# Attention beside two feed-forward layers: block differences and output sums issued at other points, loads moved, and the softmax of the later heads done by ScalarE per head

## The chip, the core and the metric

One NeuronCore of a Trainium2 chip runs one program. The metric is the device time of one execution in microseconds (us). Engines are named as the profile names them: PE (TensorE matmuls), PEld (its weight loads), DVE (VectorE), ACT (ScalarE), POOL (GpSimd), and SP, whose queue issues the DMAs of this kernel in program order.

## The reference

Chunked attention with 4 batches, 8 heads, 768 positions, head size 64. Each chunk of 32 queries sees 8 memory slots, 16 positions to the left, its own 32 and 8 to the right: 64 slots. Then two feed-forward layers over 3072 tokens with 512 features and 2048 hidden values.

```python
scores = scale * np.matmul(q_c, k_full.transpose(0, 1, 3, 2))
scores = scores - np.max(scores, axis=-1, keepdims=True)
a = np.exp(scores)
a = a / (np.sum(a, axis=-1, keepdims=True) + 1e-09)
out[:, :, c_start:c_end] = np.matmul(a, v_full)
...
h = x @ w_in;  r = np.maximum(h, 0.0);  x = (r * r) @ w_out        # first layer
...
h = x @ w_in;  g = h * np.tanh(softplus(h));  y = g @ w_out        # second layer
```

## The kernel before

**Blocks and steps.** The tokens are cut into three blocks of 1024 (`NSB`), and each layer's 2048 hidden values into eight slices (`NQ`). A step is one block times one slice, so there are 48 of them: steps 0 to 23 are the first layer, 24 to 47 the second, eight to a block. All large matrix products use a seven-product scheme (Strassen-Winograd) over 2x2 blocks: instead of eight block products there are seven, and the blocks are first combined by sums and differences (`B11`, `B21`, `B12`, `B22` give `T1` to `T4`). Every operand is split into a rounded high part and a low part, so a block product is six matmuls of 128x512.

**What a step issues.** `step(s)` writes seven products of `x` with the first weight matrix (P1, P6, P5, P2, P7, P4, P3, six matmuls each, `product`, L474) and, between them, the products of the step before with the second weight matrix: eight `unit` groups of six matmuls (L525) in the first layer, seven `product2` groups of six (L560) in the second. After each group `rest()` (L677) issues what is planned for that point. A step of the first layer has 15 such points, numbered here (step, point); point 0 follows P1, 1 P6, 2 P5, 3 and 4 units 0 and 1, 5 P2, 6 P7, 7 to 9 units 2 to 4, 10 P4, 11 P3, 12 to 14 units 5 to 7.

**PSUM and who reads it.** P1 and P2 share a bank, P6, P7 and P4 a second, P5 and P3 a third. ACT copies the result of P1 (`u1`, L735), DVE adds it to that of P6 (`u2`, L744) before P7 may add to the bank, and to that of P7 (`u3`, L763) before P4; L765, L771 and L776 make three results for the activations. P2 may start when `u1` has been copied. ACT does the activation and the rounding (L493 to L503), POOL the low part (L494). `unit` results are added to `y_t` by DVE (L549; by ACT at the first slice of a block, L547), and those of `product2` to `m_t` (L558, L581).

**Attention beside the steps.** Four pairs of 128 queries belong to each block. Pairs 0 to 3 run before step 0 (`early(p)`), pairs 4 to 7 beside steps 0 to 7, pairs 8 to 11 beside steps 8 to 15, by `plan_attention` (L638): scores at point 0 of the pair, softmax at 1 and 2, exponentials at 3, `normalize` at 5, transposes at 12, copies of them by ACT at 13, values at 16, `sums_x` (POOL) at 18 and `store_x` at 22. A pair starts 25 points after the one before it in steps 0 to 7 and 19 after it in steps 9 to 15 (L882). Softmax is a maximum and a subtraction on DVE (L369, L370), one exponential of 128x512 on ACT for each half (L376), and sums on DVE (L380). `p`'s buffer is `xt0`, `k`'s `at0`, that of `v` and `stage` is `at1`.

**Between the layers.** When the last slice of a block of the first layer is done, `sums_y` (L615) stores `B11`, `B21`, `B22` and makes `T1` to `T4` by four DVE subtractions of 128x1024 in a row (L628), which are stored too. It stands behind steps 8, 16 and 24. At step 7, 15 and 23 `load_x` reads the next block's operands and `split_x` splits them (L275, L277). In the second layer seven block sums of 128x1024 on DVE (`combine`, L586, by the list `SUMS`) make the outputs of a block: two in its last step and five in the first step of the next, at the points where `done` (L717) names them. The seven blocks of `m_t` live in `y0`, `y1` and three other buffers; each block of tokens takes new ones.

**Queues.** DMAs are issued by SP, and `later(...)` keeps a store until the next `flush()`. An instruction that waits holds up all that stands behind it on its engine, SP included.

## Time and profile before

| | |
|---|---|
| time, median of 3 runs (lowest to highest) | 1129.05 us (1128.75 to 1133.09) |
| the profiled execution, its own time | 1126.08 us |
| span of its trace, first to last instruction | 1124.2 us |
| PE busy, share of the span | 1061.5 us, 94% |
| DVE / ACT / POOL busy | 898.6 / 561.6 / 430.5 us |
| granted TensorE clock, mean | 0.987 |
| chain that ended last: PE, DVE, DMA, ACT | 65%, 14%, 6%, 3% |
| DMA | 324.94 MB, mean 289 GB/s |

PE's busy time counts matmuls that overlap, and a matmul that waits in a filled pipeline still counts, so the stretches in which PE stood idle, and what ended them, tell more than the share. A granted clock of 1.00 is 2.4 GHz.

### The profile page before, as it was taken

Reading aid. Unit: us, or ns where it says so; the run is one execution under the profiler, and the core shown is the slowest. Engines: PE = TensorE matmul, PEld = TensorE weight load, DVE = VectorE, ACT = ScalarE, POOL = GpSimd, SP = SyncE. Lnnn points to the kernel's source line nnn. Section 1 sums busy time; section 2 is a strip of 40 time slices with the busy share of each in tenths; the row PEclk is TensorE's granted clock in tenths of the full one; section 3 lists DMA queues with packets and bytes.
Section 4 is the critical chain, followed back from the end, with each engine's and each line's share of the span. In section 5 each row is a group of like instructions: output and inputs, shape, how many; then the busy total and the mean of one; then the engine's idle time right before and its main releaser. Section 6 shows DMA issues by size and latency. Waiting matters only on the chain.

```text
span 1124.2 us, 19766 instructions
## 1 busy us (share of the span) xinstructions
PE 1061.5 (94%) x7478; PEld 872.3 (78%) x7478; DVE 898.6 (80%) x1170; ACT 561.6 (50%) x879; POOL 430.5 (38%) x327
## 2 busy tenths in 40 slices
PE   5779999897799999999999999999999999999997
PEld 5758787785677887888888878888878888778885
DVE  5686889969756766578999767988888888978888
ACT  2458555546544554647656555443354444444331
POOL 1215233232223333223322244546454554545552
PEclk9998999999989999999999999999999999999999
DMA  9556867777989898969999968989979889797441
GB/s 354 216 186 269 308 228 275 259 265 268 369 316 319 306 333 298 336 237 381 374 345 328 361 225 292 316 312 324 401 247 319 308 307 371 272 315 227 158 155 75
DMA packets 192125, 324.94 MB, mean 289 GB/s; under 512 B 13344, under 2 KB 151072, under 8 KB 188192
## 3 DMA queue, kind: packets, MB, share of 16 engines
q1 hardware_dynamic: 192032, 323.69, 80.9%
q8 instruction: 60, 0.98, 0.3%
q14 instruction: 33, 0.27, 0.1%
HBM read 231.62 MB, written 92.01 MB: 288 GB/s over the span
## 4 chain that ended last, share of the span: by engine, by line
PE 65%; DVE 14%; DMA 6%; issue 4%; ACT 3%; POOL 1%; SPq 0%; DVEq 0%; ACTq 0%; POOLq 0%
PE banks L480 29%; PE banks L535 16%; PE banks L570 15%; DVE m L558 3%; PE banks L416 1%; PE banks L346 1%; DVE r L521 1%; DMA w_d<-hi 1%; DMA w2s<-w_d 1%; DVE y L549 1%; DMA w1s<-w_d 1%; DVE ty L628 1%; DVE val L157 1%; DVE val L158 1%; DVE val L154 1%
## 5 line engine op out<-in xcount | busy, mean ns | idle before, releaser
L480 PE MATMUL banks<-x,w1s 128*128 128x512 f32 x2016 | 502.2, 396 | 19.1 <-DVE u L763 7.3
L494 POOL TENSOR_TENSOR g<-r,g 128x512 fp32r<-128x512 f32 x206 | 289.6, 1412 | 523.1 <-ACT g L493 434.6
L480 PEld LDWEIGHTS banks<-x,w1s 128*128 128x128 f32 x2016 | 382.3, 191 | 104.4 <-DVE u L763 9.0
L535 PE MATMUL banks<-g,w2s 128*128 128x512 f32 x1152 | 279.7, 394 | 6.9 <-DVE y L549 6.7
L535 PEld LDWEIGHTS banks<-g,w2s 128*128 128x128 f32 x1152 | 216.7, 190 | 55.7 <-DVE y L549 8.4
L570 PE MATMUL banks<-g,w2s 128*128 128x512 f32 x966 | 239.0, 390 | 1.2 <-DVE m L558 0.6
L570 PEld LDWEIGHTS banks<-g,w2s 128*128 128x128 f32 x966 | 180.6, 188 | 41.9 <-DVE m L558 2.3
L558 DVE TENSOR_TENSOR m<-banks,m 128x1024 f32<-128x1024 f32 x144 | 173.3, 1218 | 30.5 <-PE banks L570 27.5
L493 ACT CAST g<-r 128x512 fp32r<-128x512 f32 x206 | 127.0, 621 | 31.0 <-DVE r L521 23.7
L549 DVE TENSOR_TENSOR y<-banks,y 128x512 f32<-128x512 f32 x168 | 111.4, 682 | 25.7 <-PE banks L535 25.4
L494 POOL TENSOR_TENSOR g<-more,g 128x512 fp32r<-128x512 f32 x55 | 81.8, 1492 | 77.8 <-ACT g L493 63.2
L499 ACT ACTIVATE r<-r 128x512 f32<-128x512 f32 x72 | 45.4, 631 | 69.5 <-DVE r L771 46.1
L503 ACT ACTIVATE r<-r 128x512 f32<-128x512 f32 x48 | 30.3, 632 | 75.8 <-DVE r L765 38.4
L213 ACT CAST hi<-val 128x1024 fp32r<-128x1024 f32 (+1 forms) x32 | 30.4, 951 | 71.4 <-DVE val L158 42.3
L500 ACT ACTIVATE r<-r 128x512 f32<-128x512 f32 x96 | 60.7, 633 | 3.1
L154 DVE TENSOR_SCALAR val<-val 128x512 f32<-128x512 f32 x64 | 36.7, 573 | 24.4 <-ACT val L147 24.4
L346 PE MATMUL banks<-k,q 64*32 64x64 f32 x1536 | 39.4, 255 | 16.8 <-DMA k<-k_dram 10.1
L346 PEld LDWEIGHTS banks<-k,q 64*32 64x32 f32 x1536 | 33.4, 125 | 21.5 <-issue 18.2
L158 DVE SCALAR_TENSOR_TENSOR val<-raw,val 128x512 uint32<-128x512 uint32 x64 | 47.3, 738 | 2.2
L735 ACT COPY u<-banks 128x512 f32<-128x512 f32 x48 | 27.9, 581 | 41.1 <-PE banks L480 41.0
L386 POOL TENSOR_TENSOR p<-p,sum 128x512 f32<-128x512 f32 x22 | 25.6, 1186 | 57.8 <-DVE sum L383 23.3
L416 PE MATMUL banks<-pt,v 64*64 64x32 f32 x1536 | 35.1, 249 | 11.3 <-ACT pt L404 9.8
(72 smaller groups left out, 991.4 us busy)
## 6 DMA issues: line engine op xcount, KB each, us to landing
w1s<-w_d SPq DMA_DIRECT2D x280, 256.0 KB, 5.5
w2s<-w_d SPq DMA_DIRECT2D x229, 256.0 KB, 5.4
raw<-w_dram SPq DMA_DIRECT2D x64, 512.0 KB, 5.1
w_d<-w1s SPq DMA_DIRECT2D x8, 1792.0 KB, 7.1
x<-xs_d SPq DMA_DIRECT2D x14, 1024.0 KB, 10.7
k<-k_dram SPq DMA_DIRECT2D x24, 512.0 KB, 7.3
v<-v_dram SPq DMA_DIRECT2D x24, 512.0 KB, 8.7
xt<-xt_d SPq DMA_DIRECT2D x21, 512.0 KB, 7.3
```

The costliest lines, as they stand in the source:

```text
L154: nc.vector.tensor_scalar(out=val, in0=val, scalar1=LIMIT, scalar2=-LIMIT * NEGATIVE, op0=ALU.min, op1=ALU.max)
L158: nc.vector.scalar_tensor_tensor(out=vb, in0=low, scalar=29, in1=vb, op0=ALU.logical_shift_right, op1=ALU.bitwise_or)
L346: nc.tensor.matmul(out=s4[32 * c:32 * c + 32, j, hp, :], lhsT=q_t[p][r0:r0 + 64, j, hp, 32 * c:32 * c + 32], rhs=k_t[p][r0:r0 + 64, j, hp, ...
L416: nc.tensor.matmul(out=x_ps[par][64 * h2:64 * h2 + 64, o:o + 32], lhsT=v_t[p][j][r0:r0 + 64, h2, a, c, :], rhs=pt_t[p][r0:r0 + 64, h2, j, ...
L480: nc.tensor.matmul(out=ps, lhsT=w[:, a, f:f + 128], rhs=x[:, xi, c, kk, :], start=start and i == 0, stop=stop and i == len(order) - 1, ski ...
L493: nc.scalar.copy(out=g[:, 0], in_=r)
L494: nc.gpsimd.tensor_tensor(out=g[:, 1], in0=r, in1=g[:, 0].bitcast(FP32), op=ALU.subtract)
L500: nc.scalar.activation(out=r, in_=r, func=ACTF.Square)
L535: nc.tensor.matmul(out=ps, lhsT=w[:, a, blk(f), d % 2 * 128:d % 2 * 128 + 128], rhs=g_t[s, (f, t)][:, c, :], start=i == 0, stop=i == len(o ...
L549: nc.vector.tensor_tensor(out=y, in0=ps, in1=y, op=ALU.add)
L558: engine.tensor_tensor(out=to, in0=in0, in1=in1, op=ALU.add)
L570: nc.tensor.matmul(out=bank(first + d), lhsT=w[:, a, 128 * d:128 * d + 128], rhs=g[:, c, :], start=i == 0, stop=i == 2)
```

## The change

- **Softmax of pairs 4 to 11.** DVE still takes the maximum, then makes a small tile of -scale x maximum (128x8). The subtraction, the single exponential per half and the DVE sums go; ACT does eight exponentials of 128x64 per half, straight from PSUM, with the maximum as bias and the sum as a second result. Pairs 0 to 3 keep the old form.
- **Its points.** The second half's exponentials move to point 4, `normalize` to 6, the load of `v` to 8. The pairs start 24 points apart in steps 0 to 6, and 20 apart from point (8, 10) on; their loads of `q` and `k` stand at (8, 0) and (8, 1) instead of (9, 1).
- **Between the layers.** `sums_y` is replaced by `plan_sums`: stores of `B11` and `B21` at points 5 and 9 of the block's last step, `T1` at 13, `T2`, `T4` and `T3` at points 0, 1 and 3 of the next step. `T4` and `T3` are made in place in `y`; `T1` and `T2` go to `at1`, and `at0` is no longer used. The blocks of the first layer share one pair of `y` buffers.
- **Second layer.** The block sums 5 and 6 stand one and two products later in a block's first step. In the last step sum 6 goes to POOL behind product `T3`, sum 1 moves ahead to product `T2`, and the others stand two each behind `T2`, `T1` and `T4`. The blocks `T3`, `T2`, `T1`, `T4` of `m_t` keep their buffers from block to block.
- **Weights.** The second half's rounding and its split (`r`, `l`) of the second layer's weights stand one point later in steps 8 to 14.

```diff
     def softmax(p, h2):
...
+        nc.vector.tensor_reduce(out=mx, in_=s8, axis=AX.X, op=ALU.max)
+        if early(p):
+            nc.vector.tensor_tensor(
+                out=p_t[p][:, h2], in0=s8, in1=mx.unsqueeze(2).to_broadcast([128, 8, SLOTS]), op=ALU.subtract
+            )
+        else:
+            m_neg[p, h2] = sp.tile([128, 8], FP32, tag="mneg", name="mneg")
+            nc.vector.tensor_scalar(out=m_neg[p, h2], in0=mx, scalar1=-scale, scalar2=None, op0=ALU.mult)
...
     def exps(p, h2):
...
+        m = m_neg.pop((p, h2))
+        for i in range(8):
+            nc.scalar.activation(
+                out=pr[:, i], in_=s8[:, i], func=ACTF.Exp, scale=scale, bias=m[:, i:i + 1],
+                accum_out=r_t[p][:, h2, i:i + 1],
+            )
...
-            y_t[sb, t] = pool.tile([128, KD, NB], FP32, tag=f"y{t}", name="y")
+            y_t[sb, t] = y_t[sb - 1, t] if sb else pool.tile([128, KD, NB], FP32, tag=f"y{t}", name="y")
...
-            3: lambda: (exps(p, 0), exps(p, 1), load_k(p + 1) if (p + 1) % PSB else None),
-            5: lambda: (normalize(p), load_v(p) if p > PSB else None),
+            3: lambda: (exps(p, 0), load_k(p + 1) if (p + 1) % PSB else None),
+            4: lambda: exps(p, 1),
+            6: lambda: normalize(p),
+            8: lambda: load_v(p) if p > PSB else None,
...
+        s = (sb + 1) * NQ
+        at(s, 5, lambda: later(d[:, B11], blocks()[0]))
+        at(s, 9, lambda: later(d[:, B21], blocks()[1]))
+        at(s, 13, first)
+        at(s + 1, 0, second)
+        at(s + 1, 1, fourth)
+        at(s + 1, 3, third)
...
-                for n in {T2: (0,), T1: (1, 2, 3), T4: (4, 6, 5)}.get(blk, ()):
-                    combine(sb, *SUMS[n])
+                for n in {T3: (6,), T2: (0, 1), T1: (2, 3), T4: (4, 5)}.get(blk, ()):
+                    combine(sb, *SUMS[n], engine=nc.gpsimd if n == 6 else nc.vector)
...
-                for n in {B11: (3,), B22: (4,), B21: (5,), T3: (6,)}.get(blk, ()):
+                for n in {B11: (3,), B22: (4,), T3: (5,), T1: (6,)}.get(blk, ()):
...
-                plan_w(NQ + n, 0, e, "Aa|D|d|RS|s|L||||r|l", lambda e, i: round_w2(e, i, "xt2"), split_w2, "val")
+                plan_w(NQ + n, 0, e, "Aa|D|d|RS|s|L|||||r|l", lambda e, i: round_w2(e, i, "xt2"), split_w2, "val")
...
-            start, first, period = ((0, 4, 25), (NQ + 1, 8, 19))[sb]
+            start, first, period = ((0, 4, 24), (NQ, 10, 20))[sb]
```

The first place is ACT in step 0, where pair 4's exponentials stand between the activation behind P7 and the rounding of the second weights. Lines are those of each kernel: L376 before is L389 now, L499 is L516. Before:

```order
L499 ACTIVATE r<-r 128x512
L500 ACTIVATE r<-r 128x512
L493 CAST g<-r 128x512
L376 ACTIVATE p<-p 128x512 x2
L195 CAST w2s<-val 128x1024
L499 ACTIVATE r<-r 128x512
```

Now:

```order
L516 ACTIVATE r<-r 128x512
L517 ACTIVATE r<-r 128x512
L510 CAST g<-r 128x512
L389 ACTIVATE p,sum<-banks,mneg 128x64 x16
L195 CAST w2s<-val 128x1024
L516 ACTIVATE r<-r 128x512
```

Sixteen short instructions stand where two were, ahead of the same rounding and activation.

The second place is DVE over the end of step 8 and the start of step 9: the subtractions (L628, now L673), the weight decoding (L154 to L158) and `u2` (L744, now L791). Before:

```order
L628 TENSOR_TENSOR ty<-y 128x1024
L628 TENSOR_TENSOR ty<-y,ty 128x1024
L628 TENSOR_TENSOR ty<-y 128x1024
L628 TENSOR_TENSOR ty<-y,ty 128x1024
L154 TENSOR_SCALAR val<-val 128x512
L157 TENSOR_SCALAR val<-val 128x512
L158 SCALAR_TENSOR_TENSOR val<-raw,val 128x512
L744 TENSOR_TENSOR u_3107<-banks,u_3093 128x512
```

Now (L566 is the addition to `y`, L399 and L400 are pair 8's `normalize`, which waits for ACT's sums):

```order
L673 TENSOR_TENSOR ty<-y 128x1024
L566 TENSOR_TENSOR y<-banks,y 128x512 x2
L673 TENSOR_TENSOR ty<-y,ty 128x1024
L154 TENSOR_SCALAR val<-val 128x512
L157 TENSOR_SCALAR val<-val 128x512
L158 SCALAR_TENSOR_TENSOR val<-raw,val 128x512
L399 TENSOR_SCALAR sum<-sum 128x16
L400 RECIPROCAL sum<-sum 128x16
L673 TENSOR_TENSOR y<-y,ty 128x1024
L791 TENSOR_TENSOR u_3264<-banks,u_3243 128x512
```

One of the four subtractions moved into step 8, two stay ahead of `u2`, the fourth stands behind it, and the two operations of `normalize` came in ahead of `u2`.

The third place is DVE in steps 33 and 41: the block sums (L558 `m<-m`, now L575) around `u3` (L763, now L810). Before:

```order
L558 TENSOR_TENSOR m<-m 128x1024 x3
L763 TENSOR_TENSOR u_7923<-banks,u_7838 128x512
L765 TENSOR_TENSOR more<-banks,u_7923 128x512
L558 TENSOR_TENSOR m<-m 128x1024
```

Now:

```order
L575 TENSOR_TENSOR m<-m 128x1024 x2
L810 TENSOR_TENSOR u_8024<-banks,u_7941 128x512
L812 TENSOR_TENSOR more<-banks,u_8024 128x512
L575 TENSOR_TENSOR m<-m 128x1024
```

Two sums instead of three stand ahead of `u3`.

## Rows read from the trace of the kernel before

**Rows 1.** Stretches: start:end us, length, busy us by engine, clock, DMA share, GB/s.

```profile
535.40:555.80 20.40, 20.40 (x92) 16.90 (x91) 19.07 (x32) 14.42 (x23) 7.70 (x6) 1.00 1.02 376
61.40:264.90 203.50, 187.93 (x1761) 152.23 (x1762) 169.11 (x265) 118.48 (x187) 66.70 (x54) 0.97 0.72 261
264.90:473.30 208.40, 194.59 (x1825) 159.13 (x1824) 143.21 (x226) 108.65 (x173) 64.80 (x56) 0.97 0.89 313
288.80:324.80 36.00, 28.06 (x235) 22.41 (x234) 23.43 (x34) 17.74 (x30) 6.79 (x5) 0.86 1.02 379
637.40:1086.70 449.30, 442.54 (x1940) 362.80 (x1939) 378.68 (x381) 201.99 (x315) 229.51 (x159) 1.00 0.83 291
1086.70:1124.20 37.50, 30.06 (x133) 24.58 (x131) 31.23 (x29) 7.77 (x13) 12.07 (x8) 0.96 0.15 56
```

**Rows 2.** PE in order of time, steps 0 to 8: start, us, matmuls [idle before <-ended by].

```profile
84.37 2.93 PE L480 MATMUL banks<-x,w1s 128*128 128x512 f32 x6 [4.09 <-DVE r L771]
...
137.28 0.30 PE L416 MATMUL banks<-pt,v 64*64 64x32 f32 x2 [1.89 <-ACT pt L404]
...
141.05 4.84 PE L480 MATMUL banks<-x,w1s 128*128 128x512 f32 x12
...
214.34 1.65 PE L535 MATMUL banks<-g,w2s 128*128 128x512 f32 x6 [1.70 <-DVE y L549]
...
254.51 3.02 PE L480 MATMUL banks<-x,w1s 128*128 128x512 f32 x12 [1.40 <-DVE u L763]
...
276.21 1.64 PE L480 MATMUL banks<-x,w1s 128*128 128x512 f32 x6 [1.16 <-DVE u L744]
```

**Rows 3.** Groups of instructions by line: count | busy us, mean ns | idle before.

```profile
L370 DVE TENSOR_TENSOR p<-banks,mx 128x512 f32<-128x512 f32 x24 | 16.6, 692 | 6.9 <-PE banks L346 3.6 <-DMA w1s<-w_d 1.9 <-DVE mx L369 0.6
L380 DVE TENSOR_REDUCE sum<-p 128x8 f32<-128x512 f32 x24 | 15.5, 679 | 1.6 <-ACT p L376 1.4
L382 DVE TENSOR_SCALAR sum<-sum 128x16 f32<-128x16 f32 x12 | 2.1, 175 | 0.4
L404 ACT COPY pt<-banks 128x512 f32<-128x512 f32 x24 | 12.9, 582 | 0.3 <-PE banks L394 0.3
L581 ACT COPY m<-banks 128x1024 f32<-128x1024 f32 x21 | 20.7, 1010 | 2.0 <-PE banks L570 2.0
L494 POOL TENSOR_TENSOR g<-r,g 128x512 fp32r<-128x512 f32 x206 | 289.6, 1412 | 523.1 <-ACT g L493 434.6 <-issue 73.4 <-DVE val L220 9.1
```

**Rows 4.** ACT in order of time, pair 4's exponentials in step 0.

```profile
78.47 1.15 ACT L376 ACTIVATE p<-p 128x512 f32<-128x512 f32 x2
```

**Rows 5.** DVE in order of time, pair 4's sums in step 0.

```profile
82.00 1.27 DVE L380 TENSOR_REDUCE sum<-p 128x8 f32<-128x512 f32 x2
```

**Rows 6.** SP's queue in order of time: start of issue, us, DMA.

```profile
238.24 0.33 SPq L442 DMA_DIRECT2D xt_d<-stage  x1
...
246.43 1.25 SPq L261 DMA_DIRECT2D xt<-xt_d  x2
```

**Rows 7.** PE in order of time, step 9.

```profile
300.26 1.67 PE L480 MATMUL banks<-x,w1s 128*128 128x512 f32 x6 [3.12 <-DVE u L744]
...
307.35 0.65 PE L346 MATMUL banks<-k,q 64*32 64x64 f32 x32 [2.56 <-DMA k<-k_dram]
...
313.83 0.31 PE L346 MATMUL banks<-k,q 64*32 64x64 f32 x1 [1.72 <-issue]
```

**Rows 8.** DVE in order of time, step 9: the second subtraction.

```profile
293.60 2.21 DVE L628 TENSOR_TENSOR ty<-y,ty 128x1024 f32<-128x1024 f32 x1
```

**Rows 9.** PE in order of time, steps 25 and 33.

```profile
667.99 1.65 PE L480 MATMUL banks<-x,w1s 128*128 128x512 f32 x6 [0.53 <-DVE u L744]
...
829.12 3.01 PE L480 MATMUL banks<-x,w1s 128*128 128x512 f32 x12 [2.53 <-DVE u L763]
```

**Rows 10.** DVE in order of time, step 33 and the end.

```profile
822.80 5.67 DVE L558 TENSOR_TENSOR m<-m 128x1024 f32<-128x1024 f32 x3
...
1115.49 4.61 DVE L558 TENSOR_TENSOR m<-banks,m 128x1024 f32<-128x1024 f32 x4
```

More of the change, by code (lines that the diff above doesn't have):

```diff
@@ L584, in product2, with combine @@
         add(m, ps, m)
-    def combine(sb, to, other, store=False):
+    def combine(sb, to, other, store=False, engine=nc.vector):
         m = {b: m_t[sb, b] for _, b in PRODUCTS2}
-        add(m[to], m[to], m[other])
+        add(m[to], m[to], m[other], engine)
         if store and (to, other) in SUMS[3:]:
@@ L613, in last_unit @@
         flush()
-    def sums_y(sb):
-        d = xt_d[1][sb]
-        y0, y1 = y_t[sb, 0], y_t[sb, 1]
-        b11, b21, b12, b22 = (i.rearrange("p k s -> p (k s)") for i in (y0[:, 0:2], y0[:, 2:4], y1[:, 0:2], y1[:, 2:4]))
-        nc.sync.dma_start(out=d[:, B11], in_=b11)
-        nc.sync.dma_start(out=d[:, B21], in_=b21)
-        nc.sync.dma_start(out=d[:, B22], in_=b22)
-        if sb < NSB - 1:
-            both = [pool.tile([128, 2, 2 * NB], FP32, tag=f"at{n}", name="ty") for n in range(2)]
-            t = [both[n // 2][:, n % 2] for n in range(4)]
-        else:
-            t = [pool.tile([128, 2 * NB], FP32, tag=("xt0", "xt1", "xt2", "at1")[n], name="ty") for n in range(4)]
-        for n, (t1, t2) in enumerate(((b12, b11), (b22, t[0]), (b22, b12), (b21, t[1]))):
-            nc.vector.tensor_tensor(out=t[n], in0=t1, in1=t2, op=ALU.subtract)
-            later(d[:, T1 + n], t[n])
     beside = {}
@@ L653, in plan_attention, with plan_sums, blocks, minus @@
             at(s, i + n, work)
+    def plan_sums(sb):
+        d = xt_d[1][sb]
+        t = {}
+        def blocks():
+            y0, y1 = y_t[sb, 0], y_t[sb, 1]
+            return [i.rearrange("p k s -> p (k s)") for i in (y0[:, 0:2], y0[:, 2:4], y1[:, 0:2], y1[:, 2:4])]
+        def minus(n, to, in0, in1):
+            nc.vector.tensor_tensor(out=to, in0=in0, in1=in1, op=ALU.subtract)
+            later(d[:, n], to)
+        def first():
+            b11, _, b12, _ = blocks()
+            t["both"] = pool.tile([128, 2, 2 * NB], FP32, tag="at1", name="ty")
+            minus(T1, t["both"][:, 0], b12, b11)
+        def second():
+            b22 = blocks()[3]
+            later(d[:, B22], b22)
+            minus(T2, t["both"][:, 1], b22, t["both"][:, 0])
+        def fourth():
+            b21 = blocks()[1]
+            minus(T4, b21, b21, t["both"][:, 1])
+        def third():
+            _, _, b12, b22 = blocks()
+            minus(T3, b12, b22, b12)
+        s = (sb + 1) * NQ
[5 more added lines that the diff above has]
+        at(s + 1, 3, third)
     def plan_w(s, i, e, order, round_, split, val):
@@ L788, in step @@
         flush()
-        if prev and where(s - 1)[0] == 0 and where(s - 1)[2] == NQ - 1:
-            sums_y(where(s - 1)[1])
     with tc.manual_schedule():
@@ L881, in tile_chunk_attention_moe_moe2 @@
             p = PSB * (sb + 1)
-            start, first, period = ((0, 4, 25), (NQ + 1, 8, 19))[sb]
+            start, first, period = ((0, 4, 24), (NQ, 10, 20))[sb]
             at(start, 0, lambda p=p: load_q(p))
             if sb:
-                at(start, 0, lambda p=p: load_k(p))
+                at(start, 1, lambda p=p: load_k(p))
             for n in range(PSB):
                 plan_attention(start, first + period * n, p + n)
+        for sb in range(NSB):
+            plan_sums(sb)
         for sb in range(1, 2 * NSB):
```

28 lines of the change are left out of this document (16 added, 12 removed).

## The prediction

> **What bounds the kernel now.** I read the busy times by stretch first, then PE in order of time for the gaps, then the engines named as what ended them. An undisturbed step is step 19: 20.40 us, PE busy throughout, clock 1.00 [rows 1]. It holds 90 matmuls of 128x512, so one costs 20.40/90 = 0.227 us. From that each stretch has a floor:
>
> - Steps 0 to 7 hold 672 such matmuls (step 0 has no second-layer product): 152 us. Attention adds some 264 small matmuls a pair at 0.65/32 = 0.02 us [rows 7], about 5 us. 203.5 - 172 = some 31 us are lost [rows 1].
> - Steps 8 to 15: 8 x 20.4 + 20 = 183; 208.4 were taken, so 25 are lost, and over half of that in step 9 alone, whose row has 36.00 us at a clock of 0.86 [rows 1].
> - Steps 24 to 46: 20.4 + 22 x 84 x 0.227 = 439; 449.3 were taken, so 10 are lost [rows 1].
> - The end: 132 matmuls are 30 us of 37.5 [rows 1].
>
> So PE bounds the kernel, and beside it some 75 us are waits and slow clock. The reader should see that DVE ends most of those waits: 4.09 and 1.70 us in steps 1 and 5, 1.40 to 1.16 in steps 7 and 8 [rows 2], 3.12 in step 9 [rows 7], 2.53 in step 33 [rows 9]. DVE is busy 169 of 203 us in steps 0 to 7 while ACT is busy 118 [rows 1]. The change takes work from DVE, or from before the instruction that PE waits for, and gives part of it to ACT.
>
> **The price of one short exponential.** The trace has no ACT instruction this narrow, none with a bias from a tile, none with a sum. Copies from PSUM cost 582 ns for 512 columns and 1010 for 1024 [rows 3], so 0.836 ns a column and 154 ns fixed: 64 columns are 0.21 us, the lower end. The upper end is the exponential of 512 columns, 1.15/2 = 0.58 us [rows 4], as eight times fewer columns should not take longer. I take 0.36: the lower end plus a second fixed part of 0.154 for the two added operands, since the narrow instruction is nearest to the fixed part of the copies. A half is then 2.9 us, a pair 5.8 against 1.15 before, and ACT gains 4.6 us a pair, 37 us in all.
>
> The Trainium skill's page "ScalarE: Activation LUTs", section "What ACT_TABLE_LOAD costs", states that a per-partition pointer operand adds about 93 ns to an activation and that back-to-back ones overlap by as much. By it, and nothing for the sum, an exponential would be an estimated 0.24 us and a pair 3.8; the total below would be some 3 us lower. No row here shows such an operand.
>
> **What DVE saves.** Per pair two subtractions and two sums go, 2 x (0.69 + 0.68) = 2.74 us; two small scalings come, at most 0.18 each [rows 3]: 2.4 us less, 19 over eight pairs. How much reaches PE is a matter of place.
>
> **Part by part** (negative is faster):
>
> 1. *Steps 0 and 1, +1.* Sixteen exponentials start where two did, at 78.5 [rows 4], and end near 84.3. DVE's `normalize` started at 82.0 with sums that took 1.27 [rows 5], so its next operation ran at 83.3; now it waits until 84.3. Behind it on DVE stands L771, for which PE waits at the head of step 1 [rows 2]. The saved DVE time is lost to the new wait, and 1 us more. Ends: -2 (at 0.21) and +4 (at 0.58).
> 2. *Steps 2 to 6, -2.* Three pairs save DVE 7.2 us. PE lost there 1.89 behind ACT's copies of the transposes, then about 2 at half clock (twelve matmuls in 4.84 us against 2.9), and 1.70 behind DVE with a like wait just before [rows 2]. But DVE again has `normalize`, and the weight decoding behind it, waiting for an ACT that is 4.6 us later, so I give PE a third. Ends: -7 (all of it) and +5 (4.6 us on PE's path once).
> 3. *Steps 7 and 8, -6.* The loads of block 1 were issued at 246.43, after the store of pair 7, issued at 238.24, had landed [rows 6]; the split of what they brought makes DVE late, and PE waits six times between 254.51 and 276.21, 1.40 to 1.16 us each in the first and last [rows 2], some 6 us idle and 8 with the restarts. With a period of 24 pair 7 stands three points, over 4 us, earlier. The loads then meet the weight stores of the same time, so I leave a quarter. Ends: -8 and -2.
> 4. *Step 9, -9.* Above its floor of some 23 us it lost 13: 3.12 behind `u2`, 2.56 for `k`, 1.72 within the scores on "issue", and the low clock after them [rows 7, 1]. `k` waited since its buffer held the differences and its load stood behind them in SP's queue; now it is loaded at (8, 1), into a buffer the differences don't use, ten points ahead: 2.6 and most of the clock loss go. Of the four subtractions two stay before `u2`, one at 2.21 us [rows 8], behind pair 8's exponentials on ACT, the rebias and `normalize`; I leave 2 us of that wait. SP stands at the store of `T4` until DVE has made it, and the load of `v` for pair 8 stands behind that: 1 us for it. The "issue" wait may come again anywhere in a burst of scores; 1 us for that. Ends: -13 and -4.
> 5. *Steps 10 to 18, -2.* Three pairs' DVE savings and an extra point between one pair's values and the next's scores, in a stretch that lost little outside step 9. Ends: -5 and +3.
> 6. *Step 25, -1.* PE waited 0.53 for `u2` behind the third group of subtractions [rows 9] and as long again a little later; only two stand before `u2` now. Ends: -1.5 and 0.
> 7. *Steps 33 and 41, -4.* Three block sums of 5.67/3 = 1.89 us stand before `u3`, and PE waits 2.53 for it [rows 10, 9]; step 41 shows the same. One of them moves behind: -1.9 each. Ends: -5 and -3.
> 8. *The end, -1.5.* DVE's last additions end at 1120.1, four in a row in 4.61 us [rows 10], and the stores wait for them. Two sums leave this chain, one to POOL and one to before L771, which delays two activations that the last products need. A sum is 1.2 to 1.9 us. Ends: -3 and 0. POOL's sum is at least two of its 512-wide instructions, 2 x 1.41 = 2.8 us [rows 3], beside DVE. DVE's subtraction above took 2.21 us beside POOL, where additions with one operand in PSUM took 1.15 at the end [rows 8, 10]. The skill's page "SBUF — State Buffer", section "Who interferes with whom", states that a VectorE operation with two SBUF inputs and a GpSimd operation exclude each other for a whole instruction. By that rule this term would be an estimated -0.5; the longer row agrees with it.
>
> The weights' point (`l` behind L771 in steps 8 to 14) is costed within 3 to 5: its cover is that the weights are needed a whole layer later. The stores moved from behind step 8 to points 5 and 9 cost nothing for the same reason: their readers are nine or more steps off.
>
> Sum: +1 - 2 - 6 - 9 - 2 - 1 - 4 - 1.5 = -24.5, against the profiled execution's 1126.1: 1101.6. That execution lies 3.0 below the median of the runs shown, so the median should come to 1129.05 - 24.5 = **1104.5**.
>
> **The rivals.**
>
> *ACT becomes the bound (slower).* In step 3, from the end of P4 on, ACT has pair 6's 16 exponentials, two activations of three instructions, two rebiases and the copy `u1`: 16e + 9 x 0.6 us. PE needs `u1` for P2, after P3, three units, P1, P6, P5 and two units, nine groups of 1.36 us: 12.2. It decides from e = 0.42 on. At 0.58 PE waits 2.5 us, and with DVE's wait of point 1 behind it some 3.5 a pair: 28 over eight pairs, and after a long wait PE ran at half clock for some 2 us [rows 2], in half of them 8. With the -24.5 that is +12: 1141. For it: nothing in the trace bounds the sum's cost well. Against: an exponential of 64 columns would have to cost as much as one of 512. Chance 0.08.
>
> *The attention part gives nothing.* DVE's freed time goes into waiting for ACT in every pair, and the new order in step 9 makes as many waits as it removes but that for `k`. Then points 3 (-2), 4 (-4), 6, 7 and 8 remain, -12: 1117. For it: point 1 shows the wait. Against: DVE has few idle stretches in steps 0 to 7. Chance 0.18.
>
> *Relief adds up.* If waits get short enough that the clock does not fall, points 2 to 5 reach their good ends, -7 - 8 - 13 - 5, with the rest -39: 1090. For it: the half-clock stretches follow waits. Chance 0.12.
>
> **How the numbers follow.** The forecast has the remaining 0.62. The measurement can tell about 0.5%, 5.6 us, from no change: "faster" is below 1123.4. The forecast's own case, the relief and nearly all of the second rival lie there: 0.62 + 0.12 + 0.13 = 0.87. The rest of the second rival and a mild form of the first, 0.06, lie within; 0.07 above. The range runs from the relief at 1090 to just past the second rival, 1118, and leaves out 0.08 for the first rival and a little on either side.
>
> **What would show it.** Right: short exponentials near 0.36 us; step 9 under 27 us, with no wait for `k`; waits of about 0.7 us in steps 33 and 41; loads of block 1 issued at the head of step 7; PE's wait at the head of step 1 no shorter than 4 us. Wrong: exponentials over 0.45 us and PE idle behind `u1` in the attention steps; PE waiting for `v` in step 9; new half-clock stretches in steps 2 to 13.

## The result and the profile after

| | before | after |
|---|---|---|
| time, median (lowest to highest), same chip | 1128.9 us (1127.66 to 1133.09, 4 runs) | 1111.07 us (1109.68 to 1115.53, 4 runs) |
| the profiled execution, its own time | 1126.08 us | 1109.68 us |
| span of its trace | 1124.2 us | 1107.9 us |
| DVE / ACT / POOL busy | 898.6 / 561.6 / 430.5 us | 884.5 / 588.9 / 436.7 us |
| chain that ended last: PE, DVE, ACT, DMA | 65%, 14%, 3%, 6% | 68%, 14%, 6%, 5% |

The ratio is 0.9842, with a 95% interval of 0.9805 to 0.988: 17.8 us faster by the medians, 16.3 by the spans. The forecast was 1104.5, 24.5 below the 1129.05 that it started from, with a range of 1090 to 1118. The sign was right and the time is in the range, 6.6 us above the forecast. Several terms of the sum missed in both directions, and that is the subject of what follows.

First the windows of the kernel after, by stretch, as in [rows 1]: start:end, length, busy us of PE, PEld, DVE, ACT, POOL, clock, DMA share, GB/s. They are steps 0 to 7, 8 to 15, then 7, 8, 9 and 10 alone, 24 to 46, and step 47 with the end.

```profile
59.90:256.70 196.80, 184.31 (x1761) 149.08 (x1762) 160.69 (x257) 131.88 (x307) 68.82 (x54) 0.97 0.74 269
256.70:458.90 202.20, 193.49 (x1826) 157.52 (x1825) 134.45 (x218) 121.79 (x293) 64.81 (x56) 0.98 0.91 323
232.70:256.70 24.00, 21.42 (x92) 16.59 (x91) 16.23 (x23) 12.47 (x18) 5.59 (x4) 1.00 1.03 382
256.70:283.60 26.90, 24.37 (x235) 19.01 (x234) 22.37 (x36) 16.62 (x25) 7.03 (x5) 1.00 0.89 312
283.60:310.70 27.10, 24.90 (x227) 19.64 (x226) 15.51 (x25) 16.30 (x53) 7.18 (x5) 1.00 1.04 384
310.70:340.70 30.00, 27.45 (x244) 22.78 (x243) 17.60 (x32) 20.85 (x60) 11.18 (x11) 0.89 0.87 316
623.40:1068.70 445.30, 441.94 (x1939) 362.89 (x1938) 379.08 (x381) 201.79 (x314) 229.58 (x159) 1.00 0.85 294
1068.70:1107.90 39.20, 32.18 (x133) 25.34 (x132) 32.62 (x28) 7.76 (x13) 15.38 (x9) 0.96 0.14 54
```

Against [rows 1], steps 0 to 7 are 6.7 us shorter, 8 to 15 6.2 and 24 to 46 4.0; step 47 with the end is 1.6 longer. Step 9 fell from 36.0 to 27.1 and has full clock; step 10 has a clock of 0.89. The pairs' scores that stood in step 9 stand in step 8, so steps 7 to 9 are compared as one below. Where the table gives steps, each runs from the first matmul of its P1 to that of the next.

| steps | before | after | moved | forecast (its point) |
|---|---|---|---|---|
| before step 0 | 61.4 | 59.9 | -1.5 | 0 |
| 0 and 1 | 50.8 | 49.5 | -1.3 | +1 (1) |
| 2 to 6 | 127.1 | 123.4 | -3.8 | -2 (2) |
| 7 to 9 | 85.5 | 78.0 | -7.5 | -6 - 9 (3, 4) |
| 10 to 18 | 210.6 | 210.6 | +0.1 | -2 (5) |
| 25 | 20.75 | 19.04 | -1.7 | -1 (6) |
| 33 and 41 | 44.3 | 42.0 | -2.3 | -4 (7) |
| 47 and the end | 37.5 | 39.2 | +1.6 | -1.5 (8) |

Each column is one execution, and steps move by themselves too. With the code of the changed kernel left as it was there, later executions show 59.5 to 62.2 us before step 0, 15.8 to 17.6 for step 0, and 26.3 to 29.5 for step 3, where PE waits 2 to 3 us on "issue" and then runs some matmuls at half clock. So the first row is no gain of the change, and 2 us in steps 0 to 6 prove nothing.

PE in order of time, the kernel after, as [rows 2, 7, 9]: start, us, matmuls, in brackets the idle time before them and what ended it.

```profile
81.39 2.93 PE L497 MATMUL banks<-x,w1s 128*128 128x512 f32 x6 [4.07 <-DVE r L818]
...
250.86 1.65 PE L552 MATMUL banks<-g,w2s 128*128 128x512 f32 x6 [1.54 <-DVE y L566]
...
268.09 1.65 PE L497 MATMUL banks<-x,w1s 128*128 128x512 f32 x6 [1.23 <-DVE u L791]
...
293.35 1.66 PE L497 MATMUL banks<-x,w1s 128*128 128x512 f32 x6 [1.01 <-DVE u L791]
...
304.22 2.35 PE L433 MATMUL banks<-pt,v 64*64 64x32 f32 x128 [1.08 <-DMA v<-v_dram]
...
314.80 0.33 PE L346 MATMUL banks<-k,q 64*32 64x64 f32 x8 [2.55 <-ACT stage L445]
...
318.60 5.00 PE L497 MATMUL banks<-x,w1s 128*128 128x512 f32 x12
...
812.30 3.01 PE L497 MATMUL banks<-x,w1s 128*128 128x512 f32 x12 [1.39 <-DVE u L810]
...
1090.42 12.57 PE L624 MATMUL banks<-g,w2s 128*128 128x512 f32 x46 [2.02 <-ACT g L510]
```

The wait at the head of step 1 is the old one (4.09 before). `u2` in step 9 fell from 3.12 to 1.01, `k` is no longer waited for, `u3` in step 33 fell from 2.53 to 1.39. New are 2.55 us in step 10 with twelve matmuls at half clock behind it (5.00 us), 1.08 for `v`, and 2.02 in the last step.

ACT in order of time, the kernel after: what it waited for in steps 7 to 10.

```profile
243.36 1.05 ACT L275 CAST x<-xt 128x1024 fp32r<-128x1024 f32 x1 [7.16 <-DMA xt<-xt_d]
...
278.62 1.05 ACT L213 CAST hi<-val 128x1024 fp32r<-128x1024 f32 x1 [2.15 <-DMA w_d<-hi]
...
307.21 0.59 ACT L564 COPY y<-banks 128x512 f32<-128x512 f32 x1 [2.42 <-DMA xt_d<-y]
...
309.38 1.05 ACT L213 CAST hi<-val 128x1024 fp32r<-128x1024 f32 x1 [1.58 <-DMA w_d<-hi]
...
314.17 1.07 ACT L445 COPY stage<-banks 128x512 f32<-128x512 f32 x2
```

Each row is a DMA that ACT stood for, in program order ahead of something PE needed. The chain in step 10 reads downward: the copy of `y` waits until the stored difference has left the buffer, the rounded weights wait until the other half's store has left `hi`, two activations follow, and only then comes the copy of `stage` that the scores wait for (314.80).

DVE in order of time, the kernel after: step 0, step 33, the last step, as [rows 5, 10].

```profile
80.33 0.18 DVE L399 TENSOR_SCALAR sum<-sum 128x16 f32<-128x16 f32 x1 [1.17 <-ACT p L389]
...
807.11 4.54 DVE L575 TENSOR_TENSOR m<-m 128x1024 f32<-128x1024 f32 x2
...
1083.81 1.26 DVE L575 TENSOR_TENSOR m<-m 128x1024 f32<-128x1024 f32 x1
1085.10 3.31 DVE L575 TENSOR_TENSOR m<-m 128x1024 f32<-128x1024 f32 x1
1088.34 0.68 DVE L818 TENSOR_TENSOR more<-banks,u 128x512 f32<-128x512 f32 x1
```

POOL in order of time, the kernel after, for the same two places:

```profile
808.30 2.27 POOL L511 TENSOR_TENSOR g<-r,g 128x512 fp32r<-128x512 f32 x1
...
1083.94 3.39 POOL L575 TENSOR_TENSOR m<-m 128x1024 f32<-128x1024 f32 x1
```

In step 33 the two sums beside POOL took 2.27 us each. In the last step the first, which began 0.13 us before POOL's sum, took 1.26, and the second, which began 1.16 us after it, took 3.31 and ended about 1.1 us after POOL's had (1087.33). The two together took 4.6 us.

### The profile page after: what moved, and what is told of

It reads as the page before. It is cut to its first block, busy times and chain, and to the rows that moved or that the text cites. A ratio compares the mean times of both kernels' runs of the same rounds, so it can differ in the third digit from the quotient of the medians.

```text
span 1107.9 us, 20000 instructions
## 1 busy us (share of the span) xinstructions
PE 1058.6 (96%) x7478; PEld 868.5 (78%) x7478; DVE 884.5 (80%) x1153; ACT 588.9 (53%) x1119; POOL 436.7 (39%) x328
## 4 chain that ended last, share of the span: by engine, by line
PE 68%; DVE 14%; ACT 6%; DMA 5%; issue 4%; SPq 1%; POOL 1%; DVEq 0%; ACTq 0%; POOLq 0%
PE banks L497 31%; PE banks L587 17%; PE banks L552 15%; PE banks L433 2%; DMA w_d<-hi 2%; DVE m L575 2%; ACT p L389 2%; PE banks L346 2%; DVE y L566 1%; DVE val L157 1%; DVE val L154 1%; DVE val L158 1%; DVE r L538 1%; DMA w2s<-w_d 1%; PE banks L624 1%
## 5 line engine op out<-in xcount | busy, mean ns | idle before, releaser
L575 DVE TENSOR_TENSOR m<-banks,m 128x1024 f32<-128x1024 f32 x144 | 173.4, 1217 | 31.2 <-PE banks L587 27.1
L566 DVE TENSOR_TENSOR y<-banks,y 128x512 f32<-128x512 f32 x168 | 110.7, 681 | 16.4 <-PE banks L552 16.4
L516 ACT ACTIVATE r<-r 128x512 f32<-128x512 f32 x72 | 45.5, 632 | 50.5 <-DVE r L818 27.1
L154 DVE TENSOR_SCALAR val<-val 128x512 f32<-128x512 f32 x64 | 39.2, 612 | 35.5 <-ACT val L147 35.5
L220 DVE TENSOR_TENSOR val<-val,hi 128x1024 f32<-128x1024 f32 (+1 forms) x32 | 35.8, 1118 | 27.0 <-ACT hi L213 26.7
L158 DVE SCALAR_TENSOR_TENSOR val<-raw,val 128x512 uint32<-128x512 uint32 x64 | 47.2, 737 | 2.2
L403 POOL TENSOR_TENSOR p<-p,sum 128x512 f32<-128x512 f32 x22 | 27.5, 1271 | 47.4 <-DVE sum L400 23.8
```

Source lines behind the costliest of these rows:

```text
L154: nc.vector.tensor_scalar(out=val, in0=val, scalar1=LIMIT, scalar2=-LIMIT * NEGATIVE, op0=ALU.min, op1=ALU.max)
L158: nc.vector.scalar_tensor_tensor(out=vb, in0=low, scalar=29, in1=vb, op0=ALU.logical_shift_right, op1=ALU.bitwise_or)
L516: nc.scalar.activation(out=r, in_=h, func=ACTF.Relu)
L566: nc.vector.tensor_tensor(out=y, in0=ps, in1=y, op=ALU.add)
L575: engine.tensor_tensor(out=to, in0=in0, in1=in1, op=ALU.add)
```

## The experiments

My theories after the result were: the first load of block 1 is late because DMA is full with weight stores; the end grew because of POOL's sum; the softmax gave little. Each had a rival that keeps the same totals. Single times of one kernel on one chip lie up to almost 10 us apart here, so most verdicts are read from the steps of the traces, of which each kernel has one. The kernel before had medians of 1126.73 us (first four runs), 1130.38 (next four), 1130.43 (next three) and 1128.59 (last), each on the chip of those runs.

**The end: place or POOL (two runs).** First the block sums of the last step as before:

```diff
-                for n in {T3: (6,), T2: (0, 1), T1: (2, 3), T4: (4, 5)}.get(blk, ()):
-                    combine(sb, *SUMS[n], engine=nc.gpsimd if n == 6 else nc.vector)
+                for n in {T2: (0,), T1: (1, 2, 3), T4: (4, 6, 5)}.get(blk, ()):
+                    combine(sb, *SUMS[n])
```

> The changed kernel with the block sums of the last step as they were: one sum ahead of L818's operation, the other six behind it, all on DVE. Theory (the two sums that now stand ahead of L818 take 4.6 us beside POOL's sum and delay the operation that the last gate and so PE wait for): the last step and the end go from 39.2 back to about 37.5 us, the 2.0 us wait of PE for ACT's g in the last step goes, the whole about 1109.4 us. Rival (the last step is longer for another reason, such as the clock or the weights' loads): 39.2 us stay and the wait of PE stays; the whole 1111 us.

Then the changed kernel's places, but all on DVE:

```diff
-                    combine(sb, *SUMS[n], engine=nc.gpsimd if n == 6 else nc.vector)
+                    combine(sb, *SUMS[n])
```

> The changed kernel with all block sums of the last step on DVE, in the changed kernel's places: only POOL's part is taken back. Theory (it is POOL's sum beside DVE's that costs): the sums ahead of L818 take about 1.2 us each, three in 3.6 us instead of two in 4.6, L818's operation comes about 1 us earlier, the end 38.2 us, the whole about 1110 us. Rival (it is the place, a second sum ahead of L818, that costs): three sums stand there now, L818 comes no earlier or later, the end 39 to 40.4 us, the whole 1111 to 1112 us.

Measured: 1110.0 us (ratio 0.9835, 0.9793 to 0.9877) and 1108.35 us (0.9836, 0.9804 to 0.9869). Step 47 with the end took 37.5 and 37.3 us against 39.2. Windows of the second, then its DVE and its PE in order of time:

```profile
1072.80:1110.00 37.20, 30.57 (x133) 24.36 (x131) 31.36 (x28) 7.76 (x13) 12.77 (x8) 0.97 0.15 57
```

```profile
1088.67 2.48 DVE L575 TENSOR_TENSOR m<-m 128x1024 f32<-128x1024 f32 x2
1091.08 0.68 DVE L818 TENSOR_TENSOR more<-banks,u 128x512 f32<-128x512 f32 x1
```

```profile
1093.17 0.96 PE L624 MATMUL banks<-g,w2s 128*128 128x512 f32 x3 [0.81 <-ACT g L510]
1094.54 10.04 PE L624 MATMUL banks<-g,w2s 128*128 128x512 f32 x43 [0.40 <-POOL g L511]
```

Without POOL's sum the same two DVE sums take 2.48 us instead of 4.6. Three sums now stand ahead of L818, which comes 18.3 us after the step's start (1072.8), against 19.6 (1068.7) with two. So POOL's sum made the end longer, as the second run's theory says. The places have a small price too: in the first run PE does not wait at the last products, in the second 0.81 and 0.40 us. Even so the new places, all on DVE, end 0.3 us earlier than the old ones, as fewer sums are left behind the last products.

This repeats: step 47 with the end is 37.26 us in all seven traces with the new places all on DVE, and 38.5 to 39.3 in all four with POOL's sum. The spread of those four goes with the clock. PE's wait is 2.02 us in the kernel after as in the kernel with the old softmax (below); in the latter, which took 38.5, the 43 products behind it ran in 10.08 us, while in the kernel after the granted clock fell to 0.62 and 0.52 in the two stretches of 2 us behind the wait (1090.4 to 1094.4).

**The loads of block 1: two stores put off.**

```diff
-            later((w1_d, w2_d)[kind][0][j], w.bitcast(FP32))
+            to = (w1_d, w2_d)[kind][0][j]
+            if (j, kind) in ((NQ - 1, 0), (NQ - 2, 1)):
+                at(NQ - 1, (10, 12)[kind], lambda: later(to, w.bitcast(FP32)))
+            else:
+                later(to, w.bitcast(FP32))
```

> The changed kernel with two stores of finished weights, issued at the end of step 6 just ahead of the loads of block 1, put off to points 10 and 12 of step 7. Their reader is eight steps away. Theory (the loads of block 1 land late since DMA is full with those two stores, 2.9 MB): the first load of block 1 lands about 7 us earlier against the head of step 7 (near 4 instead of 10.6 us after it), ACT's 7.2 us of waiting there shrinks, and PE's waits of some 5 us in steps 7 and 8 go down by 3 to 5 us: 1106 to 1108 us. Rival 1 (DVE has too much to do between 245 and 260 us, whenever the loads land): steps 7 and 8 stay within 1 us of 23.95 and 26.93, the whole 1111 us. Rival 2 (the stores only move and meet the loads of step 8): step 8 or 9 is longer by as much as step 7 is shorter, the whole 1110 to 1112 us.

Measured: 1111.89 us (0.9864, 0.9836 to 0.9892), so nothing in the time. Windows of this kernel, steps 7, 9 and 10:

```profile
235.80:256.60 20.80, 20.73 (x91) 16.74 (x90) 16.14 (x23) 12.42 (x18) 5.59 (x4) 1.00 0.92 303
...
283.50:313.60 30.10, 25.15 (x227) 19.51 (x226) 19.80 (x32) 19.67 (x58) 8.44 (x6) 1.00 1.04 394
313.60:339.20 25.60, 24.22 (x243) 20.14 (x242) 14.83 (x29) 18.26 (x55) 9.91 (x10) 1.00 0.90 326
```

ACT in order of time, same kernel:

```profile
239.13 1.05 ACT L279 CAST x<-xt 128x1024 fp32r<-128x1024 f32 x1
...
281.70 1.05 ACT L217 CAST hi<-val 128x1024 fp32r<-128x1024 f32 x1 [5.32 <-DMA w_d<-hi]
...
293.03 0.67 ACT L786 COPY u<-banks 128x512 f32<-128x512 f32 x1
```

The split of block 1 starts 3.3 us into step 7 instead of 10.6, without a wait, and step 7 has lost all of its stalls: the two stores had caused them. But the stores moved into the traffic of step 8. There `hi`'s buffer is freed 3.1 us later (281.70 against 278.62), and behind that cast on ACT stand two activations, then pair 8's exponentials, two instructions of the weights, then `u1`: at 293.03 against 289.96 in the kernel after. PE waits 2.61 us for it in step 9, which is 3 us longer. Step 10 is then shorter (25.6), 11 and 12 longer by 1.1 and 1.2. Both the theory (for step 7) and the second rival (for the whole) came true.

**What the softmax is worth (three runs).** Taken out of the changed kernel: in three places `if early(p)` becomes

```diff
-        if early(p):
+        if True:
```

> The changed kernel with the softmax of the later pairs as before (DVE subtracts the maximum, ACT takes one exponential a half, DVE sums), at the changed kernel's points and with its loads, block differences and block sums. Theory (the softmax saves DVE 2.4 us a pair, of which a third or less reaches PE): steps 0 to 13 take 3 to 8 us more, the whole 1114 to 1119 us. Rival (the gain of steps 0 to 15 is all by the earlier loads, the new period and the moved differences): 1110 to 1112 us. Rival 2 (sixteen short exponentials on ACT delay the rest and the softmax costs more than it saves): 1106 to 1109 us.

The kernel before with the softmax alone, that is the new `softmax` and `exps`, the sums in `normalize` for early pairs only, and

```diff
-            3: lambda: (exps(p, 0), exps(p, 1), load_k(p + 1) if (p + 1) % PSB else None),
-            5: lambda: (normalize(p), load_v(p) if p > PSB else None),
+            3: lambda: (exps(p, 0), load_k(p + 1) if (p + 1) % PSB else None),
+            4: lambda: exps(p, 1),
+            5: lambda: load_v(p) if p > PSB else None,
+            6: lambda: normalize(p),
```

> The kernel before, with the softmax by ACT passes and its points alone; loads, block differences, period and block sums stay as before. Theory (the softmax is a small part of the gain): 0 to 4 us faster than before, in steps 2 to 6 and 10 to 13, nothing in steps 7 to 9. Rival 1 (it is the larger part, and taking it out of the changed kernel did not show it because loads bounded that one): 6 to 12 us faster. Rival 2 (ACT's short exponentials delay the rest where the new points do not make room): 1 to 5 us slower.

And the old softmax in the kernel with put-off stores and no weights in step 9 (below), all block sums at the end on DVE:

> As the run before in this list, with the softmax of the later pairs as before (subtraction and sums on DVE, one exponential a half). With the changed kernel alone this gave 3 us more in the steps and nothing in the medians. Theory (DMA's fullness hid what the softmax saves on DVE): with DMA relieved the old softmax costs 4 to 8 us more, mostly in steps 2 to 6 and 9 to 13. Rival (DVE's 2.4 us a pair lie where DVE waits for ACT or for loads anyway): within 3 us.

Measured: 1111.02 us without it (0.9856, 0.9824 to 0.9888; the changed kernel 0.9842); 1128.45 with it alone (0.9991, 0.9969 to 1.0012, against 1130.38); 1107.83 in the third (0.9806, 0.9779 to 0.9833), against 1109.17 with the new softmax. Windows of the first of them, steps 0 to 7:

```profile
61.80:261.70 199.90, 183.81 (x1761) 148.98 (x1762) 168.61 (x265) 118.11 (x187) 67.35 (x54) 0.98 0.72 265
```

DVE is busy 168.6 us instead of 160.7, so it does save 7.9 us in four pairs, 2.0 a pair (2.4 were forecast), and the stretch is 199.9 us long; with the new softmax it took 196.7 to 201.9 in five executions with the same code there. Over steps 0 to 15, where all eight pairs stand, the old softmax took 3.2 us more than the new one in the first pair of traces, 3.0 less in the second and 2.2 more in the third: no common sign, and differences of a size that three executions of one code show there too (399.0 to 401.8 us). So no run shows a gain by the softmax in any of the three surroundings; the tightest, the second, leaves room for 3.5 us by its interval (0.9969).

The rest of the gain, nearly all of it, is in the other edits. The block sums and subtractions of the second layer's steps are shown: steps 33 and 41 together take 42.0 to 42.1 us and step 25 takes 19.04 in all twelve traces with the new order, against 44.3 and 20.75 in the two with the old one. The loads, the spacing of the pairs and the places of the differences all bear on steps 0 to 10 and were not run one by one; what each of them is worth there is read from the waits that went, not shown by a run.

**Work taken out of step 9 (two runs).** The weights of that step go to later ones; all block sums at the end are on DVE.

```diff
-            if n < NQ - 1:
-                plan_w(NQ + n, 0, e, "Aa|D|d|RS|s|L|||||r|l", lambda e, i: round_w2(e, i, "xt2"), split_w2, "val")
+            if n < NQ - 2:
+                plan_w(NQ + n + (n > 0), 0, e, "Aa|D|d|RS|s|L|||||r|l", lambda e, i: round_w2(e, i, "xt2"), split_w2, "val")
...
-                n -= NQ - 1
+                n -= NQ - 2
...
-                    2 * NQ + 1, 10 * n, e, "Aa|D|d|RS|s|Lr||l",
+                    2 * NQ, 5 + 10 * n, e, "Aa|D|d|RS|s|Lr||l",
```

> The changed kernel with all block sums of the last step on DVE, and with no weights prepared in step 9: that piece of work (1 MB loaded, 1.8 MB stored, some 6 us of DVE and 4 of ACT) moves one step on, and the last of the row goes to steps 16 to 22. Theory (from 275 to 315 us DMA is full, and what comes or goes lands 7 to 9 us after its issue, so that ACT's copies of y and the rounded weights wait for stores, and the scores behind them): with 2.9 MB less the stores land within 5 us, PE's waits for ACT's stage copy in step 10 and for pt in step 9 go, steps 9 and 10 take 50 to 53 us instead of 56 to 57, steps 11 to 15 stay within 1 us of 118.7, 16 to 23 at most 1 us more; the whole 1104 to 1107 us. Rival (the waits of steps 9 and 10 come from the order on ACT and DVE, whatever DMA does): 56 to 57 us stay, and so does the whole, 1108 to 1110 us. Rival 2 (the work is in the way wherever it goes): steps 11 to 23 are longer by what 9 and 10 gain.

With the two put-off stores as well:

> As the run before in this list, and with the two weight stores of step 6 put off to step 7. Theory (the put-off stores brought step 7 down by 3.1 us and came back in step 9 since DMA was full there; with less to move in step 9 they do not come back): step 7 at 20.8 us, steps 9 and 10 at most 1 us above those of the kernel without the put-off stores, the whole 1101 to 1105 us. Rival (they come back in any case, as their 2.9 MB meet the stores of y): steps 8 to 10 are longer by 3 us, the whole as without.

Measured: 1108.99 us (0.9825, 0.9787 to 0.9863) and 1109.17 (0.9828, 0.9793 to 0.9863). Windows of the first, step 9, step 10, steps 16 to 18:

```profile
291.00:314.60 23.60, 23.60 (x228) 19.64 (x227) 9.77 (x13) 16.97 (x54) 9.36 (x7) 1.00 1.01 376
314.60:338.80 24.20, 24.18 (x244) 20.18 (x243) 16.40 (x30) 16.84 (x53) 9.68 (x10) 1.00 0.87 306
458.80:528.50 69.70, 64.25 (x271) 51.24 (x270) 60.39 (x88) 43.65 (x69) 16.83 (x12) 0.98 0.94 339
```

Steps 9 and 10 have no stall left: 47.7 us instead of 56 to 57. Steps 16 to 18, where that work went, take 69.7 instead of 62.5. DMA's share in step 9 is still 1.01: full transfers alone do not stop PE, what stops it is an instruction in front of PE's supplier that waits for one. The run does not tell DVE's and ACT's part of the removed work from the transfers' part. Of its forecasts the second rival came true: steps 9 and 10 are 9.3 us shorter than in the kernel after, steps 11 to 23 are 9.0 longer, and the time is no better. In the second kernel step 7 is 20.8 and steps 9 and 10 take 52.0, 4.3 more than without the put-off stores, as its rival says; its trace has the shortest span of all (1102.9 us), its median has not followed.

**Other places for the same work (three runs).** The pairs of block 2 wider apart, all block sums at the end on DVE:

```diff
-            start, first, period = ((0, 4, 24), (NQ, 10, 20))[sb]
+            start, first, period = ((0, 4, 24), (NQ, 10, 22))[sb]
```

> The changed kernel with all block sums of the last step on DVE, and the pairs of block 2 spaced 22 points instead of 20, so that pair 9's scores stand two products further into step 10, past ACT's copy of pair 8's result. Theory (the 2.5 us wait of the scores in step 10 and the half-clock stretch behind it come from where the scores stand, after transfers made ACT late; DMA is full on either side, but PE has other work for those two products): steps 9 and 10 take 51 to 53 us instead of 56 to 57, and the waits of step 12, some 2 us, change place or go; the whole 1102 to 1106 us. Rival (DMA's fullness finds the next wait: the values or u1 of step 10 wait instead): steps 9 to 13 stay within 1.5 us of their sum, the whole 1108 to 1110 us.

The same with the put-off stores and, for block 1, the splits at

```diff
-            for o, i in enumerate((4, 6, 8, 9, 11, 13, 14)):
+            for o, i in enumerate((4, 6, 8, 9, 11, 12, 13) if sb == 1 else (4, 6, 8, 9, 11, 13, 14)):
```

> As the run before in this list, with the two weight stores of step 6 put off to step 7, and the splits of the last two blocks of block 1 one point earlier in step 7. Theory (step 7's 3.1 us are won, and the 3.4 us of waits at the head of step 8 come from splits that stand behind two activations on ACT): step 7 at 20.8, step 8 at 24 to 26 instead of 26.9, steps 9 and 10 at most 2 us above the run before; the whole 1098 to 1103 us. Rival (what step 7 wins comes back in steps 9 and 10 with the put-off stores): the whole within 2 us of the run before.

The weights of steps 9 to 14 begun later, with the put-off stores and all block sums at the end on DVE:

```diff
-                plan_w(NQ + n, 0, e, "Aa|D|d|RS|s|L|||||r|l", lambda e, i: round_w2(e, i, "xt2"), split_w2, "val")
+                plan_w(NQ + n, 6 - n if n else 0, e, "Aa|D|d|RS|s|L|||||r|l", lambda e, i: round_w2(e, i, "xt2"), split_w2, "val")
```

> The changed kernel with all block sums of the last step on DVE, the two weight stores of step 6 put off to step 7, and the weights of steps 9 to 14 begun 5 points later in step 9, 4 in step 10 and so on to none in step 14, so that their loads and stores leave the stretch in which the differences of y go out and the next ones spread over what was idle. Theory (DMA is full from 275 to 312 us only; moving traffic out of it within the same steps costs nothing later): step 7 at 20.8 us, steps 9 and 10 at 50 to 53 us, steps 11 to 15 within 1.5 us of 118.7, steps 16 to 47 at 646.6; by the steps 7 to 10 us less than the changed kernel, the whole 1101 to 1105 us. Rival (layer 1 has no room anywhere: every wait taken out of steps 9 and 10 comes back behind the pairs of steps 10 to 13, as with the wider spacing): steps 7 to 15 within 2 us of their sum in the changed kernel less the 3.1 of step 7, the whole 1107 to 1111 us.

Measured: 1112.63 us (0.9851, 0.9817 to 0.9885), 1114.36 (0.9852, 0.9816 to 0.9887), 1113.23 (0.9862, 0.9838 to 0.9887). All three theories failed, and two of the rivals were too mild. In the first, steps 9 and 10 fell to 52.5 us as the theory says, but steps 11 to 15 rose from 118.2 to 126.9; steps 9 to 13 are 1.9 us longer in sum, where the rival had 1.5. In the second, steps 9 and 10 rose again by 2.9 us, as its rival says, and the earlier splits won nothing: step 8 took 27.5 us. In the third, steps 7 to 15 are 4.5 us longer than in the kernel after, where its rival had them 3.1 shorter, within 2. ACT of the first in order of time, then its PE:

```profile
335.54 1.05 ACT L213 CAST hi<-val 128x1024 fp32r<-128x1024 f32 x1 [2.81 <-DMA w_d<-hi]
...
344.83 1.22 ACT L147 ACTIVATE val<-raw 128x512 f32<-128x512 f32 x2 [4.41 <-DMA w_d<-val]
345.95 1.07 ACT L421 COPY pt<-banks 128x512 f32<-128x512 f32 x2
```

```profile
346.58 4.12 PE L433 MATMUL banks<-pt,v 64*64 64x32 f32 x128 [4.29 <-ACT pt L421]
```

The next piece of weights waits for the store of the one before to leave `val`, the copy of the transposes stands behind it on ACT, and PE stands 4.29 us: the same chain as in step 10, one step on.

**The price of a sum.**

```diff
                 out=pr[:, i], in_=s8[:, i], func=ACTF.Exp, scale=scale, bias=m[:, i:i + 1],
-                accum_out=r_t[p][:, h2, i:i + 1],
             )
```

with DVE's two sums in `normalize` for all pairs again.

> The changed kernel with the sum of the exponentials by DVE as before and not as a second result of ACT. It leaves out nothing of the computation. What it measures: the price of the sum on ACT. Theory (the short exponential costs a fixed part and its columns, 0.29 us from start to start, and the sum is read by a second instruction that overlaps most of it): without the sum 0.20 to 0.24 us from start to start, 16 in 3.2 to 3.8 us instead of 4.63. Rival (the sum is free, the bias from a tile is what costs): 0.28 to 0.30 us as with it. DVE gets its two sums of 0.68 us a pair back; steps 0 to 13 within 2 us either way.

Measured: 1109.97 us in its one run. ACT in order of time, the kernel after, three of the 16 exponentials of pair 4:

```profile
75.46 0.31 ACT L389 ACTIVATE p<-banks,mneg 128x64 f32<-128x64 f32 x1
75.67 0.19 ACT L389 ACTIVATION_READ_ACCUMULATOR p<-banks,mneg 128x1 f32 x1
75.76 0.31 ACT L389 ACTIVATE p<-banks,mneg 128x64 f32<-128x64 f32 x1
...
76.05 0.31 ACT L389 ACTIVATE p<-banks,mneg 128x64 f32<-128x64 f32 x1
```

And without the sum, all 16 in one row with what follows them:

```profile
75.88 3.39 ACT L389 ACTIVATE p<-banks,mneg 128x64 f32<-128x64 f32 x16
79.05 1.16 ACT L195 CAST w2s<-val 128x1024 fp32r<-128x1024 f32 x1
```

With the sum one starts every 0.29 us; without it (79.05 - 75.88)/16 = 0.20, so the theory holds. The sum is read by a second instruction that mostly overlaps and adds 0.09.

## Why the prediction was right, and where its steps were wrong

The forecast named the right places: the gain lies where PE waited. It is smaller than forecast by 7.5 us in steps 7 to 9, 3.1 at the end, 2.1 in steps 10 to 18 and 1.7 in steps 33 and 41. Steps 0 to 6 gave 4.1 us more than forecast, and 1.5 came before step 0, where nothing was changed; part of that is luck, as later executions of the same code took 172.5 to 176.3 us for steps 0 to 6, against 172.8 here and 177.9 before. Two of the forecast's own signs of being wrong came: PE waits for `v` in step 9 (1.08 us, for which point 4 had left 1), and there is a new stretch at about half clock in step 10.

- **Price of the exponential.** Taken 0.36, measured 0.29. The lower end of 0.21, from the copies [rows 3], was right for all but the sum: with the bias from a tile and no sum the trace has 0.20, so no price of the bias shows. The rival in which ACT becomes the bound needed 0.42 and fell with the 0.29. By the Trainium skill's page "ScalarE: Activation LUTs", section "What ACT_TABLE_LOAD costs", the estimate was 0.24 with nothing for the sum; the trace's 0.20 without it lies below that.
- **Point 1.** The new wait of `normalize` for ACT is there, 1.17 us, and the wait at the head of step 1 is unchanged. The steps moved within what they vary by.
- **Points 2 and 5, DVE's saving.** The saving was counted about right (2.4 us a pair; 2.0 measured), and point 2 passed a third of it on to PE. The runs show nothing of it in the time. Steps 2 to 6 are shorter by the new spacing of the pairs, or by chance: with the new spacing they took 124.6 and 126.9 us with the old softmax and 122.3 to 125.6 with the new one; with the old spacing 127.1 and 125.7, old softmax and new. In steps 10 to 18 step 12 grew from 23.3 to 29.0 us while steps 13 and 14 together fell from 51.9 to 44.2, as the pairs stand elsewhere, and no gain is left. The rival "the attention part gives nothing" was right for the softmax as far as the runs can tell, and wrong for the moved scores and loads.
- **Point 3.** The step that failed is "I leave a quarter" for the weight stores of the same time. The loads were issued at the head of step 7, as forecast: at 234.74 instead of 246.43 [rows 6], 2.0 us into the step instead of 7.1. But the first split came only 1.6 us earlier in the step (10.6 us into it instead of 12.2): two stores, 2.9 MB together, stood ahead, issued at 230.13 and 233.06. SP's queue as in [rows 6], for the kernel after:

```profile
230.13 0.33 SPq L131 DMA_DIRECT2D w_d<-w1s  x1
233.06 0.33 SPq L131 DMA_DIRECT2D w_d<-w2s  x1
...
234.74 2.94 SPq L261 DMA_DIRECT2D xt<-xt_d  x2
```

  I read when a load is issued, and did not add up the bytes ahead of it. The run with the put-off stores shows that this was all in step 7: it has no stall there, and is 3.1 us shorter.
- **Point 4.** Right for `k`, for `u2` (-2.1 us) and for the clock of step 9. Wrong in that the relief stays: the copy of `y` now waits 2.42 us for a stored difference in the same buffer, since `T3` and `T4` are made in place; in the kernel before no copy of `y` waited for a DMA. By the order of ACT's rows this wait, with that for `hi`, makes the 2.55 us of step 10 and its slow clock. No run with the differences in buffers of their own tests it.
- **Points 6 and 7.** The mechanism was right; the size of 7 was not. The 1.89 us of [rows 10] is a mean of two sums of 2.31 and 2.30 beside POOL and one of 1.21 without it, in DVE's row of the kernel before:

```profile
827.25 1.21 DVE L558 TENSOR_TENSOR m<-m 128x1024 f32<-128x1024 f32 x1
```

  The two that stay ahead of `u3` still take 2.3 each, so 5.67 - 4.54 = 1.13 was won, and the wait fell by as much, from 2.53 to 1.39.
- **Point 8.** Wrong in sign. The -1.5 counted POOL's sum as time taken off DVE's chain at the end. What I did not see is the place: the sums slowed by it stand ahead of L818, whose gate the last products wait for, so PE waits 2.02 us, and its clock may fall behind that; taken back to DVE, the sum gives 1.2 to 2.0 us. By the rule of the Trainium skill's page "SBUF — State Buffer", section "Who interferes with whom", the term was an estimated -0.5. The traces agree with the rule: 1.2 us for a sum without POOL, 2.3 beside one POOL operation and 3.31 behind POOL's sum; but -0.5 has the wrong sign too, as it looks at the chain at the end alone.

What stays open is whether a second buffer for `hi` or `val` would let the gain of steps 7 to 10 stand. It was not tried. None of the versions run is faster than the changed kernel by more than the intervals: the lowest ratio, 0.9806 (0.9779 to 0.9833), overlaps 0.9842 (0.9805 to 0.988).

## What to carry to other kernels

When a load is freed from one wait, add up the bytes that are issued ahead of it: an early issue into a full DMA gains little. When an engine that works in program order stands at a store that must leave its buffer, ask what PE needs that stands behind it; moving that work elsewhere in a stage with no slack moves the wait along. And freed time on an engine is worth only what the waits that end on it are worth: DVE gained 7.9 us in four pairs, and no run shows any of it in the kernel's time. When a row gives the mean of a few instructions, look at them one by one before one of them is priced.
